# Thresholded attention with a feed-forward block: weights rebuilt from 16-bit words, loads by head, a new set of ranks

## The chip, the core and the metric

The kernel runs on one core of a Trainium2 chip. The core has a matrix engine (TensorE, called PE in the profile), a vector engine (VectorE, DVE), an engine for functions of one operand (ScalarE, ACT), a general engine (GpSimd, POOL) and an engine that here only issues transfers (SyncE, SP). Each works through its own list of instructions in the order in which the program wrote them, and semaphores hold an instruction until what it needs is there. Transfers between the device's memory and the core's on-chip memory are put into a queue by SP, ACT or POOL and carried out by 16 DMA engines that all queues share. The metric is the time of one execution in microseconds (us).

## The reference

Per batch (8) and head (8) there are q, k and v of 576 rows by 64. With scores s = q k^T / 8, a score stays where it is at least the row's maximum less tau, and is sent to -1e9 otherwise; then comes a softmax over the row and the product with v. The heads of a row are put side by side (8 x 64 = 512), which gives x of 4608 rows by 512. Then

```
h = x @ w_in            # 512 -> 2048
g = h / (1 + exp(-1.702 h))
out = g @ w_out         # 2048 -> 512
```

q, k and v are 32-bit floats. w_in and w_out come as 64-bit floats, 8 MB each, and the kernel makes 32-bit floats of them.

## The kernel before

**Attention by pairs.** Two heads make a pair; there are 32 pairs, four to a batch, counted by n. `load_qk` brings q and k of a pair (four transfers each, in runs of 32 floats), `load_v` brings v. `prep` transposes q and k on DVE. `scores` computes the transposed scores in nine tiles, `keep` copies them out of the accumulator on ACT, `in_groups` takes maxima on DVE, and `over_tiles` and `over_halves` bring these down to one value a row. `turn_rows`, `row_out` and `row_in` send that row through device memory so that it comes back on all partitions. `sub` (DVE) subtracts it, `mask` and `exps` (ACT) make the weights of the softmax, `values` and `sums_by_pe` (PE) multiply with v and with ones, `one_row`, `spread_sums` and `place_x` (DVE) divide and write x.

**Feed-forward by blocks** of 256 rows. Block 0 and 1 go first and in a plain way (`mm1_0`, `tanh`, `gelu_0`, `mm2`): mm1_0 goes through the 2048 columns of w_in in 16 steps j for each of the two blocks, four j's to a column group, and needs the pairs 0 to 3 and the four converted pieces of its column group. mm2 needs w_out. Later blocks use seven products instead of eight. From block 2 on each needs the pairs of the next batch.

**The weights.** Each matrix is 16 pieces of 128 rows by 512 columns, 512 KB as 64-bit words. `load_w` brings a piece to a staging place (SP's queue). A 64-bit float is two 32-bit words, hi and lo. DVE shifts the sign and exponent out of hi (`cv_ex`), ACT turns that into a power of two in two passes (`cv_power`, `cv_power2`), DVE cuts out the fraction of hi (`cv_frac`), joins it with lo (`cv_join`) and multiplies by the power (`cv_end`). All four DVE operations and both ACT passes are over 512 elements a partition.

**What sets the order.** Every piece of work is a `task` with an engine, a planned cost, a rank, what it comes after, and what places it takes and gives back (`limits`). `run_in_order` plays these tasks through before the kernel runs: an engine that is free takes, among its tasks that are ready and find their places free, the one with the lowest rank; and in that order the instructions are written. So nothing is decided on the chip, the plan's order is the order of each queue. A task's rank is n plus a bias for its function: `EARLY` for pairs 0 to 3, `SECOND` for 4 to 7, `LATER` for the rest, and `CV` with `W_RANK` for the weights. PE's feed-forward work has the last rank (1000), so it goes where attention has none ready. `transfer` stands for the time that a transfer takes in the plan; it is no instruction.

The rows of maxima of pairs 0 to 7 go over POOL's queue, later ones over SP's. k of pair 0 is issued on ACT's queue, all other q, k, v and weights on SP's.

The lines that matter below: L397 issues q and k, L409 v, L450 weights; L500 is prep, L510 scores, L527 keep, L533 in_groups, L641 sub, L647 mask, L651 exps, L662 values and the sums, L819 mm1_0, L801 mm2; L458, L465, L469, L476, L483 and L490 are cv_ex, cv_power, cv_power2, cv_frac, cv_join and cv_end; L626 and L635 are row_out and row_in.

Of the kernel before, what the change touches and what calls it, by code (L numbers as in the profile page):

```python
# [11 lines left out]
I32 = mybir.dt.int32  # L12
U32 = mybir.dt.uint32
# [17 lines left out]
def kernel(  # L31
# [96 lines left out]
    for x in ("raw0", "raw1", "qkT0", "qkT1", "mb"):  # L128
# [12 lines left out]
        "one_row": -13.82,  # L141
        "over_halves": 23.69,
        "over_tiles": -19.38,
        "place_x": 36.77,
        "prep": -75.13,
        "row_in": -12.15,
        "row_out": 37.49,
        "scores_run": 5.02,
        "spread_max": -15.22,
        "spread_sums": 32.66,  # L150
        "sub": -13.77,
        "sums_by_pe": 11.61,
        "turn_rows": -17.79,
        "values": 9.46,
        "w_sum": 36.74,
    }
    SECOND = {
        "exps": 48.41,
        "in_groups": 90.77,
        "keep": -52.88,  # L160
        "load_qk": 12.53,
        "load_v": 67.07,
        "mask": 27.44,
        "one_row": 59.42,
        "over_halves": 22.95,
        "over_tiles": 6.12,
        "place_x": 27.27,
        "prep": 41.33,
        "row_in": 35.7,
        "row_out": 20.9,  # L170
        "scores_run": 30.56,
        "spread_sums": -25.02,
        "sub": 67.34,
        "sums_by_pe": -4.59,
        "sums_in": 9.14,
        "sums_out": 58.99,
        "turn_rows": 12.71,
        "turn_sums": 66.39,
        "values": 56.01,
    }  # L180
    LATER = {
        "exps": 20.37,
        "in_groups": 85.93,
        "keep": 12.29,
        "load_qk": 56.34,
        "load_v": 4.91,
        "mask": 45.29,
        "over_halves": 13.04,
        "over_tiles": 11.11,
        "place_x": 43.96,  # L190
        "prep": 29.75,
        "row_in": -12.01,
        "row_out": 12.27,
        "scores_run": 19.69,
        "sub": 73.39,
        "sums_in": 27.57,
        "sums_out": 40.94,
        "turn_rows": 21.08,
        "turn_sums": 42.06,
        "values": -14.78,  # L200
        "x_sum": 62.94,
    }
# [128 lines left out]
    rebias2 = const.tile([P, 1], FP32, name="rebias2")  # L331
    JOINT = 7
# [50 lines left out]
    def own(n, *pools):  # L383
        return tuple(x + "_apart" for x in pools) if n in APART else pools
# [4 lines left out]
    def load_qk(n, which, queue):  # L389
        b, hp = divmod(n, NPAIR)  # L390
        src = (q, k)[which]
        t = home(n, f"raw{which}")
        blocks = t.rearrange("p (c d) -> p c d", d=32)
        for h in range(2):
            for j in range(2):
                rows = src[b, 2 * hp + h, :, ts(j, 32)]
                queue.dma_start(  # L397
                    out=blocks[ds(64 * h + 32 * j, 32), :, :],
                    in_=rows.rearrange("(a p t) d -> p t a d", a=2, p=32) if which
                    else rows.rearrange("(c p) d -> p c d", p=32),  # L400
                )
        raws[n, which] = t
# [24 lines left out]
    for x in HALVES + W64:  # L427
        limits[x] = 1

# [8 lines left out]
    def load_w(i):  # L438
        dst, src, c, j = pieces[i]
        dram = src[ts(c, P), ts(j, WC)]  # L440
        if not wide:
            nc.gpsimd.dma_start(out=dst[:, c, ts(j, WC)], in_=dram)
            return
        at = staged(i)
        if at in W64:
            t = arena[:, ts(W64.index(at), 2 * WC)]
        else:
            t = w_out[:, ts(HALVES.index(at), 2), :].rearrange("p a b -> p (a b)")
        t = t.bitcast(U32)
        nc.sync.dma_start(out=t, in_=dram.bitcast(U32))  # L450
        t = t.rearrange("p (c w) -> p c w", w=2)
        cv[i] = t[:, :, 1], t[:, :, 0], dst[:, c, ts(j, WC)]

    def cv_ex(i):
        hi, _, o = cv[i]
        nc.vector.tensor_single_scalar(  # L458
            out=o.bitcast(I32), in_=hi.bitcast(I32), scalar=20, op=ALU.arith_shift_right
        )  # L460

    def cv_power(i):

        o = cv[i][2]
        nc.scalar.activation(out=o, in_=o.bitcast(I32), func=AF.Prelu, bias=rebias, alpha=2.0**-40)  # L465

    def cv_power2(i):
        o = cv[i][2]
        nc.scalar.activation(  # L469
            out=o.bitcast(I32), in_=o, func=AF.Prelu, bias=rebias2, scale=2.0**23, alpha=2.0**40  # L470
        )

    def cv_frac(i):

        hi = cv[i][0]
        nc.vector.tensor_scalar(  # L476
            out=hi.bitcast(I32), in0=hi.bitcast(I32), scalar1=0x000FFFFF, scalar2=0x00100000,
            op0=ALU.bitwise_and, op1=ALU.bitwise_or,
        )

    def cv_join(i):
        hi, lo, _ = cv[i]
        nc.vector.scalar_tensor_tensor(  # L483
            out=hi.bitcast(FP32), in0=lo, scalar=2.0**-32, in1=hi.bitcast(I32),
            op0=ALU.mult, op1=ALU.add,
        )

    def cv_end(i):
        hi, _, o = cv.pop(i)
        nc.vector.scalar_tensor_tensor(  # L490
            out=o, in0=hi.bitcast(FP32), scalar=2.0**-20, in1=o, op0=ALU.mult, op1=ALU.mult,
        )
# [512 lines left out]
    nc.gpsimd.memset(rebias, -896.0)  # L1005
    nc.gpsimd.memset(rebias2, 1792.0 * 2.0**-17)
    nc.gpsimd.memset(flat[0], 0.0)
# [48 lines left out]
    W_RANK = (-17.54, -19.75, 3.69, 13.93, 26.33, -28.4)  # L1056
    W_TIME = 1.6
    ready_w, w_loads = [], []
    for i in range(len(pieces)):
        y = 0 if i < NDC else 2 if i < n_in else 4  # L1060
        n = NDC if i < NDC else n_in - NDC if i < n_in else n_in
        first = (0, 0, NDC, 0, n_in)[y]
        rank = W_RANK[y] + (W_RANK[y + 1] - W_RANK[y]) * (i - first) / n
        if not wide:
            ready_w.append(task("POOL", 1.2, rank, load_w, i, lag=2.5))
            continue
        place = (staged(i),)
# [8 lines left out]
        e = task("DVE", 0.33, rank, cv_ex, i, after=[a] + over)  # L1076
        m = task("ACT", 0.67, rank, cv_power, i, after=[e])
        m = task("ACT", 0.67, rank, cv_power2, i, after=[m])
        a = task("DVE", 0.42, rank, cv_frac, i, after=[e])
        a = task("DVE", 0.61, rank, cv_join, i, after=[a])  # L1080
        ready_w.append(task("DVE", 0.61, rank, cv_end, i, after=[a, m], give=place))
# [190 lines left out]

    for n in range(NP):
# [10 lines left out]
        cost = (2.6, 2.4, 2.9, 2.4)[n] if n < NPAIR else 2.1  # L1284
        lq = task("SP", cost, r - 2.0, load_qk, n, 0, q0, after=behind, take=own(n, "raw0"))
        lk = task(
            "SP", cost if n else 0.1, r - 2.0, load_qk, n, 1, q1, after=behind, take=own(n, "raw1"),
        )
        lq, lk = (transfer("DMS", 1.45, a, lag=1.7 if n else 3.0) for a in (lq, lk))
        v_m = f"v_m{n % 2}"  # L1290
        lv = task("SP", 3.0, r + (1.85 if n < 2 else -1.2), load_v, n, after=lvs[-1:], take=(v_m,))
        lvs.append(lv)
        lv = transfer("DMS", 1.1, lv, 1)
        pq = task("DVE", 0.69, r, prep, n, 0, after=[lq], take=own(n, "qkT0"), give=own(n, "raw0"))
        pk = task("DVE", 0.69, r, prep, n, 1, after=[lk], take=own(n, "qkT1"), give=own(n, "raw1"))
# [58 lines left out]
        elif n in BY_DMA:  # L1354
            a = task("DVE", 0.21, r, turn_rows, n, after=[a])
            a = transfer(rq[2], 0.3, task(rq[0], 0.65 * rq[1], r, row_out, n, after=[a]))
            spread[n] = task(rq[0], 1.1 * rq[1], r, row_in, n, after=[a], take=own(n, "mb"))
            m = transfer(rq[2], 0.7, spread[n], 1, give=("row",), lag=rq[3])
        else:
            m = task("DVE", 0.78, r, spread_max, n, after=[a], take=own(n, "mb"))  # L1360
# [54 lines left out]
        if n not in SUMS_BY_PE:  # L1415
# [5 lines left out]
            if n in SUMS_BY_DMA:  # L1421
# [3 lines left out]
                summed[n] = transfer(rq[2], 0.7, a, 1, give=("row_s",), lag=rq[3])  # L1425
# [43 lines left out]
```

## Time and profile before

| what | value |
|---|---|
| median of 3 runs | 1322.9 us (1321.64 to 1323.74) |
| the profiled execution | 1326.52 us |
| its span, first to last instruction | 1324.7 us |
| PE busy | 1263.5 us, 95% |
| DVE busy | 1006.5 us, 76% |
| ACT busy | 665.1 us, 50% |
| POOL busy | 236.8 us, 18% |
| moved by DMA | 87.01 MB |

The span is the stretch from the first to the last instruction of one profiled execution; a few microseconds lie around it. Busy time of an engine counts its instructions alone. A line of groups gives line, engine, operation, what is written and read, and the count; behind the bar the busy time in us and the mean of one in ns; behind the second bar the time that the engine stood idle just before these instructions and who ended it. In a window table each engine's busy time stands with its number of instructions, then the mean granted clock of PE, the DMA engines' share and the GB/s. In a list of waits the numbers are the total in us, how often, and the longest. SPq and ACTq are the issuing queues of SP and ACT; for an issue the time is how long the queue was held.

### The profile page before, as it was taken

The page shows a single profiled execution, that of the slowest core. Times are in us where ns is not written, and L with a number is a line of the kernel's source. Part 1 is how long each engine was busy: PE and PEld are TensorE (multiplying, and loading weights), DVE is VectorE, ACT ScalarE, POOL GpSimd, SP SyncE. Part 2 cuts the span into 40 slices and gives each one's busy share as a digit, 9 for nine tenths or more (in the row PEclk, how much of TensorE's full clock was granted, in tenths as well). Part 3 has the DMA queues.
Part 4 walks back from the last instruction along what each step waited for, and adds up shares of the span by engine and source line. Part 5 has one row for each costly group of instructions (what it writes and reads, how often), then busy time and mean ns, then how long its engine had stood idle before and what let it go on. Part 6 is the DMA issues. An engine that isn't in the chain of part 4 may idle for free.

```text
span 1324.7 us, 22760 instructions
## 1 busy us (share of the span) xinstructions
PE 1263.5 (95%) x9128; PEld 973.7 (74%) x9128; DVE 1006.5 (76%) x1601; ACT 665.1 (50%) x862; POOL 236.8 (18%) x276
## 2 busy tenths in 40 slices
PE   3688999899999999999999999999999999999998
PEld 1345854366777777777878877777777778888887
DVE  7798997888987888877787877777887873652642
ACT  5798494766645555555454545454655540210210
POOL 1000002112121130302121202112111217120120
PEclk9898999899999999999999999999999999999999
DMA  8725047354322212221222222221222010000000
GB/s 211 205 64 132 27 171 134 61 110 89 90 66 56 71 40 64 54 62 39 70 54 71 55 71 55 69 45 58 52 50 58 27 53 11 16 1 24 9 0 32
DMA packets 190825, 87.01 MB, mean 66 GB/s; under 512 B 159872, under 2 KB 170112, under 8 KB 190720
## 3 DMA queue, kind: packets, MB, share of 16 engines
q1 hardware_dynamic: 182560, 78.08, 23.2%
q0 software_dynamic: 5792, 7.19, 3.0%
q8 instruction: 71, 1.16, 0.4%
q10 hardware_dynamic: 2368, 0.30, 0.3%
q14 instruction: 34, 0.28, 0.1%
HBM read 71.63 MB, written 9.70 MB: 61 GB/s over the span
## 4 chain that ended last, share of the span: by engine, by line
PE 72%; DVE 13%; ACT 7%; DMA 5%; issue 2%; SPq 1%; POOL 0%; DVEq 0%; POOLq 0%
PE ops L970 23%; PE hps L779 20%; PE pv L662 8%; PE ps L510 8%; PE ps L884 4%; DVE part L533 4%; PE ps L970 4%; DVE arena L641 4%; PE ops L884 3%; ACT arena L651 3%; ACT arena L647 2%; ACT arena L527 1%; DMA arena<-row 1%; DMA arena<-row_s 1%; DMA arena<-in_k_dram 1%
## 5 line engine op out<-in xcount | busy, mean ns | idle before, releaser
L533 DVE TRANSPOSE_TENSOR_REDUCE part<-arena 128x36 f32<-128x1152 f32 (+1 forms) x295 | 357.6, 1236 | 46.9 <-ACT arena L527 35.2
L779 PE MATMUL hps<-xT,w_in 128*128 128x256 f32 x1536 | 337.0, 380 | 1.2 <-DVE arena L791 1.2
L779 PEld LDWEIGHTS hps<-xT,w_in 128*128 128x128 f32 x1536 | 290.8, 190 | 46.3 <-issue 5.3
L647 ACT ACTIVATE arena<-arena 128x1152 f32<-128x1152 f32 (+1 forms) x160 | 168.7, 1059 | 140.2 <-DVE arena L641 139.8
L527 ACT COPY arena<-ps 128x576 f32<-128x576 f32 x288 | 171.4, 645 | 119.0 <-PE ps L510 118.8
L641 DVE TENSOR_TENSOR arena<-arena 128x1152 f32<-128x1152 f32 (+1 forms) x158 | 202.0, 1325 | 14.5 <-DMA arena<-row 14.5
L510 PE MATMUL ps<-arena 64*64 64x288 f32 x2304 | 177.1, 423 | 33.7 <-DVE arena L500 23.1
L970 PE MATMUL ops<-w_out,arena 128*128 128x256 f32 x896 | 202.9, 381 | 1.8 <-DVE arena L791 1.7
L651 ACT ACTIVATE arena<-arena,shift,scl 128x1152 f32<-128x1152 f32 (+1 forms) x160 | 199.1, 1250 | 3.4
L970 PEld LDWEIGHTS ops<-w_out,arena 128*128 128x128 f32 x896 | 169.0, 190 | 29.8 <-DVE arena L791 4.1
L936 POOL TENSOR_TENSOR arena<-arena 128x256 f32<-128x256 f32 x56 | 48.3, 862 | 648.7 <-DVE arena L791 546.9
L662 PE MATMUL pv<-arena 64*64 64x288 f32 x2176 | 161.8, 407 | 0.1
L510 PEld LDWEIGHTS ps<-arena 64*64 64x64 f32 x2304 | 85.8, 138 | 101.3 <-ACT arena L527 30.0
L788 ACT ACTIVATE th<-hps 128x512 f32<-128x512 f32 x112 | 66.1, 590 | 176.2 <-PE hps L779 154.4
L970 PE MATMUL ops<-arena 128*128 128x256 f32 x672 | 150.7, 380 | 1.1 <-DVE osb L992 1.1
L970 PEld LDWEIGHTS ops<-arena 128*128 128x128 f32 x672 | 127.1, 190 | 20.8 <-issue 2.2
L662 PEld LDWEIGHTS pv<-arena 64*64 64x64 f32 x2176 | 82.3, 134 | 56.8 <-issue 11.1
L992 DVE SCALAR_TENSOR_TENSOR osb<-ops,osb 128x256 f32<-128x256 f32 x98 | 39.4, 414 | 98.0 <-PE ops L970 92.0
L791 DVE SCALAR_TENSOR_TENSOR arena<-th,hps 128x512 f32<-128x512 f32 x96 | 64.2, 669 | 38.9 <-ACT th L788 38.5
L801 PE MATMUL ops<-w_out,arena 128*128 128x512 f32 x128 | 57.1, 599 | 2.4 <-DVE w_out L490 2.4
L949 POOL TENSOR_TENSOR arena<-arena 128x512 f32<-128x512 f32 x28 | 37.6, 1347 | 109.8 <-PE ops L970 109.8
L904 ACT ACTIVATE th<-arena 128x512 f32<-128x512 f32 x32 | 20.3, 634 | 72.6 <-DVE arena L900 72.6
(117 smaller groups left out, 1088.6 us busy)
## 6 DMA issues: line engine op xcount, KB each, us to landing
arena<-in_v_dram SPq DMA_DIRECT2D x128, 144.0 KB
arena<-in_q_dram SPq DMA_DIRECT2D x128, 72.0 KB
out_dram<-osb SPq DMA_DIRECT2D x36, 256.0 KB
arena<-in_k_dram SPq DMA_DIRECT2D x124, 72.0 KB
arena<-row SPq DMA_DIRECT2D x48, 144.0 KB
arena<-row_s SPq DMA_DIRECT2D x48, 144.0 KB
w_out<-in_moe_w_in_dram SPq DMA_DIRECT2D x12, 512.0 KB
arena<-in_moe_w_out_dram SPq DMA_DIRECT2D x12, 512.0 KB
```

What stands on the lines that cost most here:

```text
L510: nc.tensor.matmul(ps[ts(c, KT), h, 0:SH], lhsT=mats[n, 1][ts(h, D), ts(j, KT)], rhs=mats[n, 0][ts(h, D), ts(c, SH)], start=True, stop=True,)
L527: nc.scalar.copy(out=sT[n, t][:, u], in_=pss.pop((n, j))[:, :, 0:SH])
L533: nc.vector.tensor_reduce(out=stats[n, op][:, t * 2 * QB : min(2 * t + 2, NK) * QB], in_=sT[n, t].rearrange("p u h (g d) -> p (u h g) d", ...
L641: engine.tensor_tensor(out=s, in0=s, in1=mbs[n].unsqueeze(1).to_broadcast(list(s.shape)), op=ALU.subtract)
L647: nc.scalar.activation(out=s, in_=s, func=AF.Prelu, alpha=STEEP)
L651: nc.scalar.activation(out=s, in_=s, func=AF.Exp, scale=scl, bias=shift)
L662: nc.tensor.matmul(o[c][ts(h, D), 0:SH], lhsT=left(j, h)[ts(c, KT)], rhs=sT[n, t][ts(c, KT), u, h, :], start=(j == 0), stop=(j == NK - 1),)
L779: nc.tensor.matmul(hidden[j][:, ts(f, BLK)], lhsT=w_in[:, c, ds((f * HF + j) * P, P)], rhs=xTs[blk][:, c, :], start=(c == 0), stop=(c == N ...
L788: nc.scalar.activation(out=ths[j], in_=hidden[j], func=AF.Tanh, scale=GELU_SCALE / 2)
L791: nc.vector.scalar_tensor_tensor(out=g[:, :, j, :], in0=two(ths.pop(j)), scalar=1.0, in1=two(hidden.pop(j)), op0=ALU.add, op1=ALU.mult,)
L884: nc.tensor.matmul(places[j, x], lhsT=left[:, c, ts(j, P)], rhs=right[:, c, :], start=(c == 0), stop=(c == 1),)
L970: nc.tensor.matmul(banks[blk][k][:, ts(o, HM)], lhsT=left[:, j, :], rhs=right[:, j, :], start=(j == 0), stop=(j == HF - 1),)
```

## The change

1. **Conversion.** A piece's 64-bit words are now also read as four 16-bit words. ACT's first pass takes the top 16-bit word (sign, exponent, four bits of fraction) directly; `cv_ex` and `cv_frac` are gone. DVE joins the second 16-bit word and lo (`cv_low`); the result is cut to 19 bits and made whole, for w_in by an ACT pass (`cv_round`, Relu), for w_out by a DVE operation (`cv_whole`); `cv_end` puts the bits together with exclusive-or and or. So a piece has two DVE operations and three ACT passes (w_in), or three and two (w_out), where it had four and two.
2. **q and k by head.** `load_qk` issues the two transfers of one head; a pair's q is two tasks, and so is its k.
3. **The plan counts what is under way.** Two new limits, `ring` (48) and `slots` (9): a weight piece takes 2 and 1, a head of q or k 18 and 2, a v 4 and 4, and they are given back when the planned transfer ends. Some planned costs change.
4. **New ranks** in all four tables and in `W_RANK`.

```diff
     EARLY = {
-        "exps": 47.12,
-        "in_groups": 31.3,
-        "keep": 32.74,
-        "load_qk": 29.52,
-        "load_v": 88.91,
-        "mask": 47.59,
-        "over_halves": 23.69,
-        "over_tiles": -19.38,
-        "prep": -75.13,
-        "row_in": -12.15,
-        "row_out": 37.49,
-        "sub": -13.77,
-        "sums_by_pe": 11.61,
+        "exps": 11.43,
+        "in_groups": -31.63,
+        "keep": -11.23,
+        "load_qk": 20.14,
+        "load_v": 19.9,
+        "mask": 171.06,
+        "over_halves": -1.59,
+        "over_tiles": -20.68,
+        "prep": -4.32,
+        "row_in": 9.72,
+        "row_out": -14.48,
+        "sub": 178.85,
+        "sums_by_pe": 312.21,
...
     SECOND = {
-        "exps": 48.41,
-        "in_groups": 90.77,
-        "load_qk": 12.53,
-        "load_v": 67.07,
-        "mask": 27.44,
-        "sub": 67.34,
+        "exps": 6.76,
+        "in_groups": 291.18,
+        "load_qk": 165.77,
+        "load_v": 335.03,
+        "mask": 337.17,
+        "sub": 17.25,
...
     CV = {
-        "cv_end": 47.56,
-        "cv_ex": 38.81,
-        "cv_frac": 65.22,
-        "cv_join": 80.5,
-        "cv_power": 48.25,
-        "cv_power2": -13.93,
-        "load_w": 28.32,
+        "cv_end": 5.42,
+        "cv_low": -24.3,
+        "cv_power": 173.78,
+        "cv_power2": -24.9,
+        "cv_round": -14.9,
+        "cv_whole": -11.38,
+        "load_w": 330.13,
     }
...
-    def load_qk(n, which, queue):
+    def load_qk(n, which, queue, h):
...
-        for h in range(2):
-            for j in range(2):
+        for j in range(2):
...
+    limits.update(ring=48, slots=9)
...
-    def cv_ex(i):
-        hi, _, o = cv[i]
-        nc.vector.tensor_single_scalar(
-            out=o.bitcast(I32), in_=hi.bitcast(I32), scalar=20, op=ALU.arith_shift_right
-        )
     def cv_power(i):
-        o = cv[i][2]
-        nc.scalar.activation(out=o, in_=o.bitcast(I32), func=AF.Prelu, bias=rebias, alpha=2.0**-40)
+        top, _, _, o = cv[i]
+        nc.scalar.activation(out=o, in_=top, func=AF.Prelu, bias=rebias, alpha=2.0**-40)
...
+    def cv_low(i):
+        _, mid, lo, _ = cv[i]
+        nc.vector.scalar_tensor_tensor(
+            out=lo.bitcast(FP32), in0=lo, scalar=2.0**-32, in1=mid, op0=ALU.mult, op1=ALU.add
+        )
+    def cv_round(i):
+        lo = cv[i][2]
+        nc.scalar.activation(
+            out=lo.bitcast(I32), in_=lo.bitcast(FP32), func=AF.Relu, bias=full, scale=-8.0
+        )
+    def cv_whole(i):
+        lo = cv[i][2]
         nc.vector.tensor_scalar(
-            out=hi.bitcast(I32), in0=hi.bitcast(I32), scalar1=0x000FFFFF, scalar2=0x00100000,
-            op0=ALU.bitwise_and, op1=ALU.bitwise_or,
+            out=lo.bitcast(I32), in0=lo.bitcast(FP32), scalar1=8.0, scalar2=2.0**19 - 1,
+            op0=ALU.mult, op1=ALU.min,
         )
+    def cv_end(i):
+        _, _, lo, o = cv.pop(i)
         nc.vector.scalar_tensor_tensor(
-            out=o, in0=hi.bitcast(FP32), scalar=2.0**-20, in1=o, op0=ALU.mult, op1=ALU.mult,
+            out=o.bitcast(I32), in0=lo.bitcast(I32), scalar=2**19 - 1 if i in ROUND_BY_ACT else 0,
+            in1=o.bitcast(I32), op0=ALU.bitwise_xor, op1=ALU.bitwise_or,
         )
...
-    W_RANK = (-17.54, -19.75, 3.69, 13.93, 26.33, -28.4)
+    W_RANK = (175.06, 5.72, 196.05, 310.62, 82.78, -16.51)
     W_TIME = 1.6
+    ROUND_BY_ACT = range(n_in)
+    RING = [("ring",) * x + ("slots",) * y for x, y in ((2, 1), (18, 2), (4, 4))]
...
-        a = task("SP", 0.65, rank, load_w, i, after=w_loads[-1:], take=place)
+        a = task("SP", 0.55, rank, load_w, i, after=w_loads[-1:], take=place + RING[0])
         w_loads.append(a)
-        a = transfer("DMS", W_TIME, a, 2)
+        a = transfer("DMS", W_TIME, a, 2, give=RING[0])
...
+    def two_loads(n, which, cost, r, queue, behind, take):
+        ys, a = [], None
+        ring = RING[1] if queue is nc.sync else ()
+        for h in range(2):
+            a = task(
+                "SP", cost, r, load_qk, n, which, queue, h,
+                after=behind + ([a] if h else []), take=ring if h else tuple(take) + ring,
+            )
+            ys.append(transfer("DMS", 1.25, a, lag=1.5 if n else 1.7, give=ring))
+        return ys
```

`W_RANK` holds a first and a last rank for the first four pieces of w_in, for its other twelve, and for the sixteen of w_out; in between the rank goes in equal steps. The bias of `CV` is added to it.

More of the change, by code (lines that the diff above doesn't have):

```diff
@@ L156 @@
+        "sub": 178.85,
+        "sums_by_pe": 312.21,
+        "turn_rows": -14.38,
+        "values": -19.56,
+        "w_sum": -20.0,
     }
     SECOND = {
-        "exps": 48.41,
-        "in_groups": 90.77,
-        "keep": -52.88,
-        "load_qk": 12.53,
-        "load_v": 67.07,
-        "mask": 27.44,
[L164 to L170, printed above, removed]
@@ L180 @@
+        "place_x": 0.09,
+        "prep": -16.41,
+        "row_in": 205.66,
+        "row_out": 181.09,
+        "scores_run": 21.47,
+        "spread_sums": -6.66,
+        "sub": 17.25,
+        "sums_by_pe": 334.76,
+        "sums_in": -21.09,
+        "sums_out": 5.24,
+        "turn_rows": 184.92,
+        "turn_sums": -18.91,
+        "values": -19.14,
     }
     LATER = {
[L182 to L201, printed above, removed]
+        "exps": 208.23,
+        "in_groups": 342.52,
+        "keep": -7.99,
+        "load_qk": 197.24,
@@ L202 @@
+        "load_v": -11.46,
+        "mask": 344.07,
+        "over_halves": -19.6,
+        "over_tiles": 19.84,
+        "place_x": 181.51,
+        "prep": 208.92,
+        "row_in": -6.54,
+        "row_out": -30.86,
+        "scores_run": -0.21,
+        "sub": 200.03,
+        "sums_in": 338.15,
+        "sums_out": 7.27,
+        "turn_rows": 167.17,
+        "turn_sums": 343.8,
+        "values": -25.3,
+        "x_sum": -9.1,
     }
     CV = {
-        "cv_end": 47.56,
-        "cv_ex": 38.81,
@@ L331 @@
     rebias2 = const.tile([P, 1], FP32, name="rebias2")
+    full = const.tile([P, 1], FP32, name="full")
     JOINT = 7
@@ L393, in load_qk @@
         blocks = t.rearrange("p (c d) -> p c d", d=32)
-        for h in range(2):
-            for j in range(2):
[L396 to L400, printed above, removed]
-                )
+        for j in range(2):
+            rows = src[b, 2 * hp + h, :, ts(j, 32)]
+            queue.dma_start(
+                out=blocks[ds(64 * h + 32 * j, 32), :, :],
+                in_=rows.rearrange("(a p t) d -> p t a d", a=2, p=32) if which
+                else rows.rearrange("(c p) d -> p c d", p=32),
+            )
         raws[n, which] = t
@@ L1075 @@
         ]
[L1076 to L1080, printed above, removed]
+        m = task("ACT", 0.67, rank, cv_power, i, after=[a] + over)
+        m = task("ACT", 0.65, rank, cv_power2, i, after=[m])
+        a = task("DVE", 0.61, rank, cv_low, i, after=[a])
+        if i in ROUND_BY_ACT:
+            a = task("ACT", 0.65, rank, cv_round, i, after=[a])
+        else:
+            a = task("DVE", 0.43, rank, cv_whole, i, after=[a])
         ready_w.append(task("DVE", 0.61, rank, cv_end, i, after=[a, m], give=place))
@@ L1283 @@
         behind = [spread[n - 2]] if n >= NPAIR and n - 2 not in ROWS_BY_POOL else preps[n - 1 if n > 3 else n - 2] if n in (2, *range(4, NP)) else []
[L1284 to L1289, printed above, removed]
+        lq = two_loads(n, 0, 1.15, r - 2.0, q0, behind, own(n, "raw0"))
+        lk = two_loads(n, 1, 1.15 if n else 0.05, r - 2.0, q1, behind, own(n, "raw1"))
         v_m = f"v_m{n % 2}"
-        lv = task("SP", 3.0, r + (1.85 if n < 2 else -1.2), load_v, n, after=lvs[-1:], take=(v_m,))
+        lv = task("SP", 2.45, r + (1.85 if n < 2 else -1.2), load_v, n, after=lvs[-1:], take=(v_m,) + RING[2])
         lvs.append(lv)
-        lv = transfer("DMS", 1.1, lv, 1)
-        pq = task("DVE", 0.69, r, prep, n, 0, after=[lq], take=own(n, "qkT0"), give=own(n, "raw0"))
-        pk = task("DVE", 0.69, r, prep, n, 1, after=[lk], take=own(n, "qkT1"), give=own(n, "raw1"))
+        lv = transfer("DMS", 2.3, lv, 1, give=RING[2])
+        pq = task("DVE", 0.69, r, prep, n, 0, after=lq, take=own(n, "qkT0"), give=own(n, "raw0"))
+        pk = task("DVE", 0.69, r, prep, n, 1, after=lk, take=own(n, "qkT1"), give=own(n, "raw1"))
         preps.append([pq, pk])
```

54 lines of the change are left out of this document (21 added, 33 removed).

## The prediction

> **What bounds the kernel now.** I read the page's busy shares and its forty slices first: TensorE (PE) is at 95% of the span, and all its weak slices but a few tenths lie in the first five, so this change can win only the time in which PE stands still early. A window table cut at four events of the trace puts that in numbers: 16.43 is the first matmul, 60.26 the moment when pair 1's row of maxima lands, 122.25 the first feed-forward matmul (L819; I call this moment F), 286.60 the first matmul of block 2.
>
> ```profile
> core 0: us, PE busy (x) PEld busy (x) DVE busy (x) ACT busy (x) POOL busy (x), PEclk, DMA share, GB/s
> 0.00:16.43 16.43, 0.00 (x0) 0.00 (x1) 9.64 (x19) 7.04 (x10) 2.77 (x20) 1.00 0.85 185
> 16.43:60.26 43.83, 30.61 (x360) 15.06 (x360) 33.86 (x52) 30.15 (x42) 4.22 (x8) 0.88 0.92 236
> 60.26:122.25 61.99, 48.25 (x648) 26.08 (x648) 56.61 (x104) 55.92 (x70) 2.26 (x4) 0.86 0.31 77
> 122.25:286.60 164.35, 155.92 (x1037) 97.05 (x1034) 147.76 (x240) 105.47 (x141) 18.49 (x30) 0.98 0.43 105
> 286.60:1324.70 1038.10, 1028.73 (x7089) 835.54 (x7087) 758.65 (x1190) 466.56 (x601) 209.01 (x214) 1.00 0.20 50
> ```
>
> To see: before F PE is busy 78.9 of 122.25 us (43.4 idle), between F and block 2 it misses 8.4, in the remaining 1038 us 9.4. From 60 us to F VectorE (DVE) and ScalarE (ACT) are both nine tenths busy, so there the attention of pairs 1 to 3 and the weight conversion fill both engines. After F the feed-forward work fills every gap of PE, and the length is F plus what follows: what moves F moves the end, as long as PE finds work afterwards. The waits of PE up to F say what it stood for:
>
> ```profile
> PE ps L510 <- DVE arena L500: 23.1, 2, 16.4
> PE den L662 <- ACT arena L651: 17.3, 7, 5.9
> PE ps L510 <- ACT arena L527: 2.5, 2, 1.5
> ```
>
> The 16.4 is the first transpose, which waits for q and k of pair 0. The timeline of the queue on SyncE (SP) shows why they are late:
>
> ```profile
> 0.75 1.81 SPq L450 DMA_DIRECT2D w_out<-in_moe_w_in_dram  x4
> 2.61 11.68 SPq L397 DMA_DIRECT2D arena<-in_q_dram  x8
> 14.33 2.79 SPq L397 DMA_DIRECT2D arena<-in_k_dram  x4
> 17.16 1.11 SPq L450 DMA_DIRECT2D arena<-in_moe_w_in_dram  x2
> ```
>
> Four weight pieces (2 MB) go first, then eight q transfers need 11.68 us to be issued at all, where four elsewhere need 2.2; in order behind them stands k of pair 1. For the conversion the groups by line up to F, durations in ns behind the comma:
>
> ```profile
> L533 DVE TRANSPOSE_TENSOR_REDUCE part<-arena 128x36 f32<-128x1152 f32 x16 | 21.1, 1346 | 0.9 <-ACT arena L527 0.8
> L490 DVE SCALAR_TENSOR_TENSOR w_in<-w_out,w_in 128x512 f32<-128x512 f32 x8 | 5.5, 692 | 2.2 <-ACT w_in L469 1.7
> L483 DVE SCALAR_TENSOR_TENSOR w_out<-w_out 128x512 f32<-128x512 uint32 x8 | 5.4, 690 | 0.1
> L458 DVE TENSOR_SCALAR w_in<-w_out 128x512 int32<-128x512 int32 x12 | 4.6, 422 | 4.8 <-DMA w_out<-in_moe_w_in_dram 4.8
> L476 DVE TENSOR_SCALAR w_out<-w_out 128x512 int32<-128x512 int32 x12 | 4.5, 420 | 0.1
> L465 ACT ACTIVATE w_in<-w_in,rebias 128x512 f32<-128x512 int32 x14 | 10.0, 713 | 3.3 <-DVE w_in L458 3.3
> L469 ACT ACTIVATE w_in<-w_in,rebias 128x512 int32<-128x512 f32 x13 | 9.4, 724 | 2.6 <-issue 2.2
> ```
>
> **The profiled execution** took 1326.5 us: span 1324.7 and 1.8 around it. The median of the three runs is 1322.9, 3.6 lower; the sum is made on the profile and moved by that.
>
> **1. Conversion.** A piece costs DVE 0.42 + 0.42 + 0.69 + 0.69 = 2.22 us and ACT 0.71 + 0.72 = 1.43 now. After, a w_in piece costs DVE two scalar_tensor_tensor (cv_low, cv_end) and ACT a third pass; a w_out piece costs DVE a third operation, the one-source cv_whole. None is in the trace with 16-bit operands; all 512-element rows of the conversion lie between 0.42 and 0.72 us, and I take for each the row of its form: 0.69 for the two-source ones (L483 already reads every second word and mixes types), 0.42 for cv_whole, 0.72 for cv_round. So w_in: DVE 1.38 (ends 0.84 and 1.44), ACT 2.15; w_out: DVE 1.80, ACT 1.43. Over 32 pieces DVE loses 16 x 0.84 + 16 x 0.42 = 20 us, ACT gains 16 x 0.72 = 11.5 us. On the path to F lie only the pieces done ahead of it.
> The Trainium skill, ScalarE: Activation LUTs, section Rules for kernel authors, says that relu, min and mul belong on VectorE; the rows here agree (0.42 against 0.72). By that rule the third pass would better stay on DVE: four pieces less 2.9 us on ACT and plus 1.7 on DVE, the sum would be 1306 instead of 1309; it is a rule against this part of the change, and the slower rival below is the mechanism in which it would show.
> The new Relu may or may not be in the function table that is loaded once now (ACT_TABLE_LOAD, 1.28 us); if not, 16 passes with a load before and after cost up to 41 us on ACT, if it is, nothing. I take nothing, since Prelu, Copy, Exp and Tanh already share one load, and give the other end 3 in 100. The same page, section Table sets, says that relu is in every set; no run here shows it yet.
>
> **2. The first loads.** By the new ranks load_w of w_in has 378 to 631 on SP, load_qk of pairs 0 to 3 about 18 to 21 and load_v 21 to 23: q and k of pair 0 go out first and the weights fill gaps. So q's four issues run from 0.75 to about 3.4 (0.65 each); k's, on ACT's queue, now stand behind the first conversion pass and start at 5.26, after it behind the table load and one tiny operation, at 2.25, and end at 4.9 (0.67 each). Before, k landed at 11.8 by the chain (5.26 + 6.53), 3.7 after its last issue ended; keeping 3.7 gives 8.6. The last of the two transposes (0.78) makes 9.4 for the first matmul: 7.0 earlier. Ends: 0 (nothing gained if the transfers wait for one another as now) and 9. A by-product: four conversions that ran in the dead time 4.8 to 15 lose that cover; their 4 x 1.38 on DVE and 4 x 2.15 on ACT move into ACT's and DVE's gaps up to 60 us (10 of 43.8 us idle on DVE, 13.7 on ACT), and into the full stretch if those gaps close.
>
> **3. Load by head, and the planner's counting.** Same DMAs, same bytes; no instruction waits more than before. Each head's two transfers are placed apart, and the plan lets go out no more than about two heads of q and k (18 of 48 each) and nine transfers at once, so that SP isn't held for 11.68 us with k of pair 1 behind. Priced inside step 2 and 4. Behind SP in that stretch stand loads only; the row transfers of pairs 0 to 7 use POOL's queue, whose trip of pair 1 (48.95 to 60.26, 11.3 us) ran at a DMA share of 0.92, and gains or loses with that.
>
> **4. The ranks up to F.** Now pair 0's sub (bias -13.8) beats over_halves (+23.7) and row_out (+37.5) of pair 1, so pair 1's row leaves only at 48.95 and ACT waits 4.4 us in all for sub. After, sub (+179) and mask (+171) come behind all maxima and rows, so pair 1's trip runs under pair 0's sub: 2 us of the 4.4 (ends 0 and 4.4). The price is that pair 0's sub can wait for the in_groups of pairs 1 to 3 (6.1 us a pair: 4 x 1.35 + 0.74); that is bounded by the loads. The conversion falls behind attention: 27 of ACT's passes (19.4 us) lay ahead of F, four pieces suffice for the first column group (mm1_0 needs four pieces per four j), 12 x 0.72 = 8.6. Of the difference of 10.8 I take 5, since passes that run in gaps were free already (ends 0 and 10.8). PE's work ahead of F (1008 matmuls, 4 pairs whole and the scores of two more) I take as unchanged; each pair of scores less there is 72 x 0.06 (16 take 0.97 us at full clock) = 4.4 us moved behind F.
> F: 122.25 - 7 - 2 - 5 = 108.
>
> **5. From F to block 2.** DVE has 164.35 - 147.76 = 16.6 us free. It saves 16 x 0.42 = 6.7 on w_out, and gets up to 7 more w_in pieces (now 5 of 16 end behind F, then up to 12): 7 x 1.38 = 9.7. So 3 us more in a free 16.6: nothing. ACT gets 12 x 2.15 = 25.8 instead of about 7, in 58.9 free. The ends: -8.4 (all PE waits there go) and +10 (most of the free DVE time turns out not to be usable). I take 0.
>
> **6. The rest.** Ranks of pairs 8 to 31 change order only; PE misses 9.4 us in 1038, 3.6 of it after the last matmul. I take 0, ends -4 and +6.
>
> Sum: 1326.5 - 14 = 1312.5 for the profiled execution, less 3.6: 1309.
>
> **Rivals.** (a) *The weights come late, the end is slower.* cv_power has the rank 349 for piece 0, and 370 to 475 for pieces 4 to 15, behind the masks of pairs 0 to 3 (174) and of pairs 4 to 7 (341 on); load_w is last on SP. Where ACT has no gaps, group 2 of w_in is converted after the masks and exps of pair 4 or 5 (4 x 1.16 + 0.67 + 4 x 1.35 + 0.87 = 11.6 us a pair), while PE, which needs a group each 13.9 us (L819 takes 55.6 for four), stands in mm1_0. Two pairs ahead cost 23 us: 1309 + 23 = 1332. It decides from 14 us of waits on. For it: ACT at 90% ahead of F, and three passes a piece. Against: ACT waits 17.5 us for scores up to F, which takes 12 pieces' passes, and the DMA share is 0.31 from 60 us on, so loads aren't short. (b) *The start comes earlier, F hardly.* ACT needs 82 us at least ahead of F, and pair 0's sub waits for the maxima of pairs 1 to 3; then only 4 us are left: 1319. For it: both engines full from 60 us to F; against: 20 to 25% idle before. (c) *The gain is given back at block 2*, because DVE, 90% busy from F on, has the attention of pairs 4 to 7 (in_groups +291, mask +337) last: PE waits there for what it won, 1323.
>
> **Chances.** Forecast 0.48, (a) 0.28, (b) 0.14, (c) 0.07, a table load 0.03 (with (a) on the slower side). No change that can be measured is within 0.2%, 2.6 us. Forecast and (b) are faster: 0.62; (c) is the same: 0.07; (a) and the table load are slower: 0.31. The likeliest case's own range is 1298 to 1318 (F from 97 to 117: the ends of steps 2 and 4 never all together). The range over the cases is 1298 to 1333: it leaves out the slower half of (a), 0.14, and some 0.05 below.
>
> **What would show it.** Right: the first matmul near 9 us, k of pair 0 issued on ACT's queue near 2.3, no SP issue group of over 6 us in the first 30, pair 1's row sent before pair 0's sub, L819's counterpart starting near 108, DVE's sum 20 us lower and ACT's 11 higher, one ACT_TABLE_LOAD. Wrong: waits of mm1_0 (hps) on cv_end of w_in, waits of the first matmuls of block 2 on place_x, cv_low or cv_end above 0.8 us, a first matmul still near 16.

## The result and the profile after

The changed kernel takes 1299.56 us (median; 1299.39 to 1300.33), beside 1323.32 us for the kernel before: ratio 0.9823, 95% interval 0.9806 to 0.9840, so 21 to 26 us less. Its profiled execution took 1299.66 us (span 1297.9), where that of before took 1326.52 (span 1324.7). That execution of before lay 3.2 above its kernel's median, so the 26.8 us by which the two profiles differ are some 3 more than the 23.8 by which the medians do.

The window table of the changed kernel, cut at the same events as before: the first matmul (9.06), the first feed-forward matmul F (108.59), the first matmul of block 2 (260.73).

```profile
core 0: us, PE busy (x) PEld busy (x) DVE busy (x) ACT busy (x) POOL busy (x), PEclk, DMA share, GB/s
0.00:9.06 9.06, 0.00 (x1) 0.00 (x1) 1.47 (x3) 1.49 (x2) 2.80 (x21) 1.00 0.80 149
9.06:108.59 99.53, 71.20 (x1009) 39.17 (x1009) 91.58 (x144) 90.27 (x119) 6.28 (x12) 0.90 0.62 157
108.59:260.73 152.14, 152.14 (x1037) 96.29 (x1033) 135.09 (x217) 116.61 (x155) 18.43 (x30) 1.00 0.45 115
260.73:1297.90 1037.17, 1028.95 (x7089) 837.48 (x7087) 758.05 (x1191) 469.36 (x603) 213.05 (x214) 1.00 0.21 51
```

PE does the same number of matmuls in each part (1008 or 1009 ahead of F, 1037 up to block 2), so the three parts can be compared directly. F came 13.7 us earlier, the stretch from F to block 2 became 12.2 us shorter, and the rest 0.9: together 26.8 of span. Not all of that is idle time of PE: it stood 61.2 us before and stands 45.6 now, 15.6 less; the other 11.2 are its own busy time, 1263.5 before and 1252.3 now for the same 9128 matmuls. By parts its idle time fell by 6.0, 8.4 and 1.2, its busy time by 7.7 (78.9 to 71.2), by 3.8 and, in the last part, not at all. In the middle part PE is now busy throughout, at a granted clock of 1.00 instead of 0.98. DVE is busy 12.7 us less there, and its idle time is as before, 17.1 beside 16.6.

What PE still waits for up to F, from the list of waits:

```profile
PE den L666 <- ACT arena L655: 17.9, 8, 13.4
PE ps L514 <- DVE neg L1035: 9.1, 1, 9.1
PE ps L514 <- DVE arena L504: 6.1, 1, 6.1
PE ps L514 <- ACT arena L531: 4.0, 4, 1.4
```

The 16.4 of the first transpose became 9.1 (the list names a small operation that ran beside the transposes). mm1_0 (L823) waits for nothing. The first rows of the SP queue's timeline show the new order of the loads:

```profile
0.75 2.34 SPq L399 DMA_DIRECT2D arena<-in_q_dram  x4
3.14 3.08 SPq L411 DMA_DIRECT2D arena<-in_v_dram  x4
6.26 2.29 SPq L399 DMA_DIRECT2D arena<-in_q_dram  x4
8.60 0.79 SPq L453 DMA_DIRECT2D w_out<-in_moe_w_in_dram  x1
9.43 2.39 SPq L411 DMA_DIRECT2D arena<-in_v_dram  x4
11.86 3.14 SPq L399 DMA_DIRECT2D arena<-in_k_dram  x4
```

No load holds the queue for 11.68 us any more (the longest row up to F is 6.03, for a k at 46.43), and the first weight piece goes at 8.60. The main groups of the conversion, over the first 300 us, ns behind the comma:

```profile
L472 DVE SCALAR_TENSOR_TENSOR arena<-arena 128x512 f32<-128x512 uint32 x16 | 10.9, 687 | 1.9 <-DMA arena<-in_moe_w_out_dram 1.9
L493 DVE SCALAR_TENSOR_TENSOR w_in<-w_out,w_in 128x512 int32<-128x512 int32 x12 | 8.1, 683 | 1.1 <-ACT w_in L465 1.1
L486 DVE TENSOR_SCALAR arena<-arena 128x512 int32<-128x512 f32 x12 | 5.1, 432 | 0.3
L461 ACT ACTIVATE w_in<-w_out,rebias 128x512 f32<-128x512 int16 x12 | 9.2, 762 | 1.8 <-DMA w_out<-in_moe_w_in_dram 1.8
L479 ACT ACTIVATE w_out<-w_out,full 128x512 int32<-128x512 f32 x12 | 8.8, 768 | 0.0
L1029 ACT ACT_TABLE_LOAD x1 | 1.3, 1283 | 0.7 <-PEq L1469 0.7
```

L472 is cv_low, L493 cv_end, L486 cv_whole, L461 cv_power from the 16-bit word, L479 cv_round. Over the whole kernel DVE is busy 20.3 us less (1006.5 to 986.2) and ACT 12.6 more (665.1 to 677.7).

### The profile page after: what moved, and what is told of

Its sections match the earlier page's. It is cut to its first block, busy times and chain, and to the rows that moved or that the text cites. A ratio compares the mean times of both kernels' runs of the same rounds, so it can differ in the third digit from the quotient of the medians.

```text
span 1297.9 us, 22745 instructions
## 1 busy us (share of the span) xinstructions
PE 1252.3 (96%) x9128; PEld 972.9 (75%) x9128; DVE 986.2 (76%) x1553; ACT 677.7 (52%) x878; POOL 240.6 (19%) x277
## 5 line engine op out<-in xcount | busy, mean ns | idle before, releaser
L514 PE MATMUL ps<-arena 64*64 64x288 f32 x2304 | 172.1, 413 | 19.5 <-DVE neg L1035 9.1
L940 POOL TENSOR_TENSOR arena<-arena 128x256 f32<-128x256 f32 x56 | 51.8, 925 | 647.1 <-DVE arena L795 544.0
L795 DVE SCALAR_TENSOR_TENSOR arena<-th,hps 128x512 f32<-128x512 f32 x96 | 64.3, 670 | 37.4 <-ACT th L792 37.0
L908 ACT ACTIVATE th<-arena 128x512 f32<-128x512 f32 x32 | 20.3, 635 | 72.6 <-DVE arena L904 72.6
L953 POOL TENSOR_TENSOR arena<-arena 128x512 f32<-128x512 f32 x28 | 37.4, 1340 | 106.7 <-PE ops L974 106.6
```

What stands on the lines that cost most here:

```text
L514: nc.tensor.matmul(ps[ts(c, KT), h, 0:SH], lhsT=mats[n, 1][ts(h, D), ts(j, KT)], rhs=mats[n, 0][ts(h, D), ts(c, SH)], start=True, stop=True,)
L795: nc.vector.scalar_tensor_tensor(out=g[:, :, j, :], in0=two(ths.pop(j)), scalar=1.0, in1=two(hidden.pop(j)), op0=ALU.add, op1=ALU.mult,)
```

## The experiments

Because a plan fixes every queue's order, two kinds of run are kept apart: runs whose order is kept instruction by instruction, and runs that are planned anew. Times are medians; the changed kernel is 1299.6, the kernel before 1323.3 to 1324.3 in the four sets of runs, so that a difference of 1 us between runs of different sets says nothing.

**The new operations in the old order.** cv_ex issues nothing, cv_frac and cv_join issue the new cv_low and cv_whole, all in the kernel before. Here all pieces are rounded by DVE, so DVE is busy 12.3 us less over the kernel, not 20.3 as in the changed kernel.

```diff
     def cv_ex(i):
-        hi, _, o = cv[i]
-        nc.vector.tensor_single_scalar(
-            out=o.bitcast(I32), in_=hi.bitcast(I32), scalar=20, op=ALU.arith_shift_right
-        )
+        pass
```

> The kernel before with its plan, and so every queue's order, unchanged; only the conversion's operations are the new ones (all pieces rounded by VectorE: 0.69 + 0.42 + 0.69 = 1.80 us a piece instead of 2.22, ScalarE as before). VectorE loses 32 x 0.42 = 13 us. Theory A (the end moves with F, the first feed-forward matmul, and then with what VectorE carries up to block 2): F by 1 to 3 us, the stretch behind it by 0 to 6, so 1315 to 1322. Theory B (only the order counts): 1323. Theory C (the conversion is the gain): near 1305.

Measured 1321.28 us, ratio to before 0.9975 (0.9964 to 0.9986). F is 119.68 (2.6 earlier), the stretch to block 2 161.42 (2.9 shorter). So the operations, in the order of the old ones, are worth 0.25%: all three numbers lie where theory A put them, not B or C. DVE is busy 6.5 us less between F and block 2, and that stretch got only 2.9 shorter.

**The old conversion, planned with the new ranks, loads and count** (cv_ex, cv_frac and cv_join with the biases -24.3, -14.9 and -14.9).

```diff
-        m = task("ACT", 0.67, rank, cv_power, i, after=[a] + over)
-        m = task("ACT", 0.65, rank, cv_power2, i, after=[m])
-        a = task("DVE", 0.61, rank, cv_low, i, after=[a])
...
+        e = task("DVE", 0.33, rank, cv_ex, i, after=[a] + over)
+        m = task("ACT", 0.67, rank, cv_power, i, after=[e])
+        m = task("ACT", 0.67, rank, cv_power2, i, after=[m])
+        a = task("DVE", 0.42, rank, cv_frac, i, after=[e])
+        a = task("DVE", 0.61, rank, cv_join, i, after=[a])
```

> The changed kernel with the conversion of before (four VectorE operations, two ScalarE passes), planned anew with the new ranks, loads by head and the count. A: the first matmul stays near 9 us, F comes 2 to 5 us later than 108.6, and the stretch from F to block 2, where VectorE is now busy 135 of 152 us, gets some 12 us more on VectorE and becomes longer by 3 to 10: 1305 to 1314. B: 1300. C: near 1320.

Measured 1329.28 us, ratio to before 1.0040 (1.0026 to 1.0054): slower than before, outside all three expectations. The first matmul is at 8.72 and F at 116.42, still 5.8 earlier than before; but the stretch to block 2 grew to 173.89:

```profile
0.00:116.42 116.42, 75.01 (x1008) 42.09 (x1008) 101.22 (x170) 90.76 (x118) 9.20 (x33) 0.88 0.61 151
116.42:290.31 173.89, 159.95 (x1032) 97.91 (x1032) 148.78 (x241) 115.11 (x149) 21.94 (x32) 0.95 0.48 112
```

PE stands 13.9 us there. What was won ahead of F was lost, and more, behind it.

**The new ranks alone**, in the kernel before (tables and W_RANK exchanged; cv_ex, cv_frac and cv_join with the same biases).

> The kernel before with the new ranks alone: conversion, loads by pair and planned costs as before, nothing counted. A: the first matmul near 9 to 11 us, since q and k of pair 0 go first, but SP is held by pairs of loads as before, so pair 1 comes later; 1308 to 1318. B: 1300 to 1304. C: 1323.

Measured 1332.22 us, ratio 1.0062 (1.0043 to 1.0081); first matmul 8.94, F 115.98, then 176.65 us to block 2. A miss for all theories, of the same shape: earlier F, longer stretch behind it. The ranks alone make the kernel slower. Loads by head, the count and the changed planned costs make 3 us of difference between this run and the last, less than a new plan moves by itself (below), so their own worth stays open.

**The old ranks** in the changed kernel (all four tables and W_RANK).

```diff
-    W_RANK = (175.06, 5.72, 196.05, 310.62, 82.78, -16.51)
+    W_RANK = (-17.54, -19.75, 3.69, 13.93, 26.33, -28.4)
```

> The changed kernel with the old ranks (cv_low with cv_join's, cv_round and cv_whole with cv_frac's): new conversion, loads by head, count. A: the weights go first again, so the first matmul is back near 14 to 16 us; F 115 to 120; 1308 to 1318. B: 1323. C: 1300 to 1305.

Measured 1315.78 us, ratio 0.9933 (0.9914 to 0.9953): inside A's range, but not in A's way. The weights go first again (first matmul 17.47), and F, which A put at 115 to 120, is at 125.96, later than in the kernel before. The time is won behind it: the stretch to block 2 is 153.63 and the rest 1032.31, 10.7 and 5.8 shorter than before. 14 of the 16 pieces of w_in are done ahead of F (8 in the changed kernel), but DVE is busy 146.4 us in that short stretch, nearly the 147.8 of before, so other work moved into it. An order can thus leave DVE 7 us idle there instead of 17.

**DVE nearly as long as before, order kept.** Ahead of each cv_end, DVE writes a word of the staged piece that nothing reads any more, twice for w_in and once for w_out. That brings DVE's busy time to 1002.5 us, 16.3 of the 20.3 that the change took off.

```diff
     def cv_end(i):
         _, _, lo, o = cv.pop(i)
+        hi = words.pop(i)[:, :, 1].bitcast(I32)
+        for _ in range(2 if i in ROUND_BY_ACT else 1):
+            nc.vector.tensor_single_scalar(
+                out=hi, in_=lo.bitcast(I32), scalar=1, op=ALU.arith_shift_right
+            )
```

> The changed kernel with its plan and every order kept; cv_end is preceded by VectorE operations that write a dead word (two for a w_in piece, one for a w_out piece, 0.42 us each), so that the conversion is again as long on VectorE as before: 16 x 0.84 + 16 x 0.42 = 20 us. Theory D (from F to block 2 VectorE is the bound, and the conversion's gain lies there): F 108.6 plus 2 to 4, the stretch to block 2 152 plus 6 to 14, so 1308 to 1318. Theory E (the old conversion in the new order lost its 30 us because the plan came out otherwise, not because of VectorE's time): 1300 to 1303.

Measured 1313.33 us, ratio 0.9913 (0.9894 to 0.9933): 13.8 us above the changed kernel, with no order changed. Theory D's time and stretch came (F moved 4.4, a little more than its 2 to 4), E's time didn't. But E isn't ruled out for the rest: the old conversion in the new order lost 29.7, and 13.8 of these come with DVE's time alone; the other 16 are left to the plan.

```profile
0.00:112.94 112.94, 74.00 (x1008) 41.86 (x1008) 98.27 (x162) 92.49 (x121) 9.32 (x33) 0.89 0.62 150
112.94:273.85 160.91, 154.71 (x1037) 95.40 (x1034) 145.60 (x245) 116.83 (x155) 18.52 (x30) 1.00 0.42 107
```

DVE's busy time is 5.2 us higher ahead of F and F is 4.4 later; it is 10.5 higher up to block 2 and that stretch is 8.8 longer, with PE idle for 6.2. On both sides 83% of what DVE gets comes out as length, although it shows 15 to 17 us of idle time in the second stretch. Up to F, 2.8 of the 4.4 us are busy time of PE (74.0 for the 71.2 of the changed kernel), for the same matmuls at a granted clock of 0.89 instead of 0.91.

**Rounding by VectorE, planned anew.** `ROUND_BY_ACT = ()`.

> The changed kernel with all pieces rounded by VectorE (cv_whole for w_in too, planned anew): VectorE + 16 x 0.42 = 6.7 us, ScalarE - 16 x 0.72 = 11.5 us. D: ahead of F ScalarE is 97% busy (65.2 of 67 us), so F comes up to 3 us earlier, but the stretch behind it, with VectorE busier, gets 0 to 5 longer: 1297 to 1303. By the rule that a min belongs on VectorE: 1296 to 1298.

Measured 1316.46 us, ratio 0.9942 (0.9928 to 0.9956): a miss, far worse than either said. F is at 111.89, the stretch behind it 165.13. Since this run also has a new order, it was repeated with the order kept.

**Rounding by VectorE, order kept.** cv_round, at its place in the plan, issues DVE's multiply and min instead of ACT's Relu, and cv_end takes the 0 that it takes for w_out.

```diff
     def cv_round(i):
...
-        nc.scalar.activation(
-            out=lo.bitcast(I32), in_=lo.bitcast(FP32), func=AF.Relu, bias=full, scale=-8.0
-        )
+        nc.vector.tensor_scalar(
+            out=lo.bitcast(I32), in0=lo.bitcast(FP32), scalar1=8.0, scalar2=2.0**19 - 1,
+            op0=ALU.mult, op1=ALU.min,
+        )
```

> The changed kernel with every order kept, but the rounding of the w_in pieces done by VectorE at the place where ScalarE had it: VectorE + 16 x 0.42 = 6.7 us, ScalarE - 16 x 0.72 = 11.5. F+rest: ahead of F ScalarE loses up to ten passes, F by -4 to 0; behind it VectorE gets 2.5 us more in a stretch where 20 us of it on top cost 8.8: 1296 to 1301. The run that planned this anew came to 1316.5; S: the plan. If VectorE's queue is what the rounding stands in: 1302 to 1306.

Measured 1302.73 us, ratio 0.9838 (0.9823 to 0.9852): 3.2 above the changed kernel, in the range for the case that the rounding stands in DVE's queue, above that of F+rest.

```profile
0.00:111.88 111.88, 74.39 (x1009) 40.93 (x1009) 96.84 (x158) 86.57 (x111) 9.10 (x33) 0.90 0.65 153
111.88:264.63 152.75, 152.75 (x1036) 96.73 (x1033) 137.09 (x223) 112.85 (x148) 18.59 (x30) 1.00 0.45 116
```

F is 3.3 later although ACT has 5.2 us less to do ahead of it and DVE only 3.8 more; the stretch behind is 152.75, nearly the 152.14 of the changed kernel. The last scores ahead of F show how; the first line is the changed kernel, the second this run:

```profile
107.46 1.20 PE L514 MATMUL ps<-arena 64*64 64x288 f32 x16 [0.20 <-DVE xT L768]
109.75 2.20 PE L515 MATMUL ps<-arena 64*64 64x288 f32 x16 [1.84 <-DVE xT L769]
```

Until 104 us the matmuls are up to 1.4 later than in the changed kernel. DVE, which has had nine roundings by then, starts the last place_x ahead of F at 108.74 instead of 106.45; PE waits 1.84 us for it instead of 0.20, and the 16 matmuls after this wait take 2.20 instead of 1.20. Over the whole stretch up to F PE's idle time didn't grow (37.5 beside 37.4); the 3.2 us are busy time, 74.4 for 71.2. So in this order a pass less on ACT brings F no sooner, and one more in DVE's queue delays it: the ACT pass is the cheaper place, though it takes 0.77 us where DVE takes 0.41.

**Weights first, planned anew** (700 off the rank of load_w for the first four pieces of w_in).

> The changed kernel with the first four weight pieces at the head of SP's queue, as before the change. If the earlier start is worth what it moved (7.4 us): first matmul near 16, F 112 to 116, 1303 to 1307. If conversion in the dead time makes up for it: 1299 to 1301.

Measured 1329.57 us, ratio 1.0042 (1.0032 to 1.0053), F 136.97: outside both expectations, and again mixed with a new order. So this too was repeated with the order kept.

**Weights first, order kept.** The first q load issues the first four pieces ahead of itself, and load_w issues nothing for them later; everything else keeps its place.

```diff
     def load_qk(n, which, queue, h):
+        for i in range(NDC):
+            load_w(i)
```

> The changed kernel with the order of every engine kept, but the first four weight pieces put at the very head of SP's queue. Theory F+rest: the first matmul moves from 9 to about 15 us, F by the same 5 to 7, the end too: 1304 to 1307. If pair 1's trip or a full ScalarE sets F anyway: F by 0 to 3, 1299 to 1302. The run that planned this anew came to 1329.6; S puts most of that on the plan, R on the weights.

Measured 1308.02 us, ratio 0.9877 (0.9862 to 0.9891). The first matmul is at 15.56, 6.5 later; F is 6.55 later; the stretch behind F is the same to 0.01:

```profile
0.00:115.14 115.14, 71.24 (x1008) 39.23 (x1008) 93.06 (x147) 91.67 (x121) 9.10 (x33) 0.91 0.63 147
115.14:267.29 152.15, 152.15 (x1036) 96.29 (x1033) 135.38 (x217) 116.68 (x155) 18.42 (x30) 1.00 0.45 116
267.29:1304.70 1037.41, 1029.01 (x7089) 837.51 (x7087) 758.49 (x1191) 469.58 (x603) 211.42 (x214) 1.00 0.22 51
```

The end moves with the first matmul, one for one (span + 6.8). The median is 8.5 higher than the changed kernel's, a little above the expected 1304 to 1307; the profile explains 6.8 of it. No conversion moves ahead of the first matmul, so the earlier weights make up for nothing here.

**sub and mask early for pairs 0 to 3, planned anew** (biases -13.77 and 47.59).

> The changed kernel with the old biases of sub (-13.8) and mask (47.6) for pairs 0 to 3, so that pair 0's sub goes ahead of other pairs' maxima and rows. The prediction's step 4 gave that order 2 us: F 110 to 113, 1301 to 1305. If the order of sub and maxima doesn't matter, since the rows arrive when they arrive: 1299 to 1300.

Measured 1322.06 us, ratio 0.9982 (0.9970 to 0.9993), F 118.49 and then 162.07: outside both expectations, and nearly all of the gain gone, much more than the 2 us of the prediction's step 4. How much of it is the order of sub and how much the rest of the new plan, this run can't say.

**A hair's change of the plan.** Two runs move one planned cost and nothing that is computed: keep from 0.55 to 0.56, and in_groups from 1.30 to 1.31.

> The changed kernel with one planned cost moved by a hair (keep 0.55 to 0.56), which changes nothing that is computed and no rank, but lets the plan come out in another order. Theory S (the ranks fit this one order; any new plan loses what was found by search): 1305 to 1320, F later than 111, waits of TensorE up to block 2. Theory R (the ranks are good by what they put first; the losses of the runs with weights first and with sub first are those rules' prices): 1299 to 1302.

> As the run with keep's cost, a second point: in_groups planned at 1.31 instead of 1.30. S: 1305 to 1320. R: 1299 to 1302.

Measured 1309.64 us (0.9896; 0.9879 to 0.9913) and 1300.81 us (0.9825; 0.9810 to 0.9839). The second changed the order of PE in a handful of places and of SP and POOL in none, and behaves as the changed kernel; so it hardly tests the two theories. The first reordered all queues, and lost 10 us:

```profile
0.00:111.31 111.31, 72.50 (x1008) 40.73 (x1008) 94.39 (x148) 93.18 (x123) 9.08 (x33) 0.91 0.62 151
111.31:267.68 156.37, 153.51 (x1037) 95.62 (x1034) 143.55 (x226) 125.72 (x163) 18.44 (x30) 1.00 0.48 118
```

F is 2.7 later and the stretch to block 2 is 4.2 longer. So theory S holds for one point: the ranks suit this one plan, and a plan from the same ranks and nearly the same costs loses 10 us. This is why the six runs with a new plan (old conversion, ranks alone, old ranks, rounding by VectorE, weights first, sub early) can't be read as prices: each of them holds a change and a new plan, and one new plan without a change cost 10 us. How the ranks were found isn't known.

## Why the prediction was right, and where not

It forecast 1309 with a range of 1298 to 1333 and faster with 0.62; the time was 1299.56. The direction and the main chain were right, the size was short: 14 us of gain on the profile, where 26.8 came.

**What bounds it (F plus what follows): shown where the order is kept.** The run with the weights first and the order kept moved the first matmul by 6.5, F by 6.55 and the span by 6.8. Between orders F by itself decides little: the stretch behind it went from 152 to 177 us.

**Step 1, prices of the new operations: right** for DVE (0.687, 0.683 and 0.432 for 0.69, 0.69 and 0.42), about 0.05 low for the ACT passes that are new (0.75 to 0.78 for 0.71 and 0.72). DVE lost 20.3 us in all as worked out. One table load of 1283 ns stands in the trace, as before, so the rival of 3 in 100 is out. The Trainium skill, ScalarE: Activation LUTs, section Table sets, has relu in every set, and the trace agrees. The Trainium skill's rule on the same page that min and mul belong on VectorE (section Rules for kernel authors) was right by the durations (0.41 us beside 0.77) and wrong by the time: following it for all of w_in with the order kept cost 3.2 us, where step 1 had worked out a gain of 3 by it from four pieces, because DVE's queue was the one that PE waited for just ahead of F.

**Step 2, the first loads: right, with two misses that cancel.** 9.06 for 9.4 forecast; 7.4 us, of which 6.5 belong to the weights' place in the queue by the run with the order kept. k of pair 0 was issued on ACT's queue at 0.89, not 2.25, beside the table load, and its issues ended at 3.69 instead of 4.9; but both transposes (7.57 to 9.01), not only the last, still came after the loads.

**Step 3: no issue row of over 6 us in the first 30, as said** (the longest is 4.22), but what the count or the loads by head bring alone wasn't separated.

**Step 4, the ranks up to F: the sum was right, its mechanism wrong.** F came at 108.59, forecast 108. The 7 us beyond the start were put down to 5 us of fewer ACT passes and 2 us of earlier rows. But ACT's busy time ahead of F hardly moved, 93.1 to 91.8, and 26 passes (8 cv_power, 8 cv_power2, 10 cv_round) stood where 27 had been. DVE's fell from 100.1 to 93.1, and giving DVE 5.2 us back with the order kept moved F by 4.4. Nor did PE wait less: from its first matmul to F it stood 27.0 us before and 28.3 now. The 6.3 us that F gained behind the first matmul lie in PE's busy time, 7.7 less for the same 1008 matmuls, at a granted clock of 0.90 where it had been 0.88 and 0.86 in its two parts. No term of the sum was for that, so that it came out at 108 was luck in part. Pair 1's row did go out before pair 0's sub (33.57 against 37.02), as the ranks say.

**Step 5, F to block 2: the step that failed.** It put 3 us more work on DVE in that stretch, took DVE's 16.6 us of idle time as cover for it and put the length at no change, with an end of -8.4. The stretch became 12.2 shorter. First, DVE's work there fell by 12.7: the conversion takes 33.8 us there instead of 41.0, because of w_in only 8 cv_end lie behind F (8 x 0.68 = 5.5 us) and no cv_low, where the step had up to 12 pieces with both (16.6); the other 5.5 are other work, most of which now lies ahead of F. Second, DVE's idle time was no cover: it stayed at 17 us while its work and the stretch shrank together, and with the order kept 10.5 us more on DVE made the stretch 8.8 longer. Of these 17 us 6.9 are waits for rows of maxima, 3.0 for copies by ACT, 1.9 for weights; in a fixed order such gaps lie where they lie, though another order used them better (the run with the old ranks). All PE waits there went (8.4), and with them the clock's losses: the same 1037 matmuls took 3.8 less, which no term of the sum had.

**Step 6: right**, 0.9 for 0.

**From profile to median: wrong by 3.5.** The sum took the profiled execution of before to lie 3.6 above the median and the new one to do the same; it lay 0.1 above. So of the 12.9 us by which the profile was missed, 3.5 were hidden.

**The rivals.** (a), weights late in mm1_0, didn't come: L823 waits for nothing, and 5.2 us less on ACT ahead of F brought no earlier F. (b) and (c) didn't come either. But (c)'s mechanism, the gain given back between F and block 2, is just what the old conversion does under the new ranks: F 116.42 and then 173.89, 1329 us.

**Where the 26.8 us came from**, as far as runs with the order kept show it: 6.8 from the weights' place in the first loads and 14 from DVE's shorter conversion (16.3 of its 20.3 us given back). That the two may be added is assumed. The remaining 6 aren't shown: some 3 are the profiled execution of before, slower than its median, and the rest may be the order, the loads by head or the last 4 us of DVE. The worth of the operations hangs on the order: in the old one 12.3 us less on DVE were worth 3.0.

## What to carry to other kernels

Where an order written out beforehand feeds strict queues, price an engine's work by a run that keeps the order and makes that engine longer, and not by its idle time: DVE at 86 to 89% busy passed on 83% of what it was given in the new order, while in the old order 12.3 us less on it gave 3.0. Compare PE's busy time too, and not only its waits: here 11.2 of 26.8 us were the same matmuls done in less time. Ranks belong to the operations and costs with which they are used; taken alone they made this kernel slower, and a planned cost moved by 2% lost 10 of 24 us, so a comparison that plans anew needs a neutral new plan beside it.

## What wasn't expected of the hardware

An ACT pass over 512 elements that reads every fourth 16-bit word took 752 to 778 ns by group, one that reads 32-bit words side by side 713 to 725; DVE's two-operand form read the 16-bit words at no extra cost (687 against 689 with 32-bit words). An operation on ACT in place over every second word (cv_round, 768 and 772 ns) had about the same extra. Just ahead of F, 16 matmuls of one form took 1.20 us after a wait of 0.20 and 2.20 after one of 1.84; the granted clock in the last 4 us up to F was 1.00 in the first case and 0.72 in the second. So a wait of PE can cost more than its length.
